# Linear attention with an ELU feed-forward behind it: one written order for the whole kernel, Strassen's products from block 2 on, blocks 8 and 9 transposed by DMA, block 0's keys loaded in long rows, products that nobody reads

## The chip, the cores and the metric

The kernel runs on one core of a Trainium2 chip. A core has a matrix engine (PE in the profile, with its weight loads as PEld), a vector engine (DVE), a scalar engine (ACT), a general engine (POOL) and a synchronising engine (SP), each with its own instruction stream that runs in order, and 16 DMA engines that all of them share. POOL's loads convert from fp32 to fp16 on the way. The metric is the device time in microseconds (us) of one execution; lower is better.

## The reference

Two things are computed one after the other. The first is attention with an exponential decay per head, in blocks of 64 tokens with a running state; q, k and v are 4 batches x 8 heads x 768 tokens x 64.

```python
for b in range(nb):                                   # 12 blocks of 64 tokens
    intra = einsum('bhic,bhjc->bhij', qb, kb) * Dmask
    intra = einsum('bhij,bhjd->bhid', intra, vb)
    inter = einsum('bhid,bhde->bhie', qb * lam_pow, kv_state)
    out[:, :, sl] = intra + inter
    kv_state = lam_block * kv_state + einsum('bhsd,bhse->bhde', kb * rev_pow, vb)
```

The second takes the 3072 x 512 result x and computes

```python
h = x @ w_in                                          # 512 -> 2048
g = where(h > 0, h, exp(min(h, 0)) - 1)
return g @ w_out                                      # 2048 -> 512
```

Both stages are fused: as soon as a block's attention is ready, its feed-forward can start.

## The kernel before, in words

The work is cut into 24 steps, numbered s: step s handles one block of 64 tokens for two batches, so 128 rows. "Block" in this document is such a step. Two blocks that follow each other form a group of 256 rows, 12 groups in all.

A block's attention is issued by `visit(so, us, ss, sx)`, which puts work of up to four blocks into the PE stream: for block ss the scores (`mm_S`), for us the update of the state (`mm_U`), for so the output (`mm_I` from the state in two halves, with a drain and the semaphore `crossed` between them, and `mm_O` from the scores), and for sx the transposes of q and k (`mm_T`, or the loop over `qn` and `kn` below it for the blocks under `NQ`, 6). Around it stand `att_C` (copies the transposed q and k from PSUM into the tile T), `att_P` (scores times mask), `att_N` (new state), `att_X` (attention output into xt), and three products with the decay: `decay_v` (tile vd), `decay_s` (sd) and `decay_q` (qs). From block `NT`, 10, on, the transposes are made by `dma_T` on SP's queue instead: two DMA transposes for a block, into one of two TD buffers.

The feed-forward's first product is cut into units (`mm1_h`) of one PSUM bank each, 8 matmuls of 256 columns or 16 of 128, into one of two banks psH. A unit's ELU is made by ACT (two activations, tiles e and r) and DVE (one operation, into g). The second product has two forms. `mm2` multiplies a block's g by w_out directly: 16 matmuls of 512 columns in four calls; it serves blocks 0 to 5. From group 3 on (block 6), Strassen's scheme takes 7 products for the two blocks of a group in place of 8 (`product_of`, called by `part`): each product is 8 matmuls of 256 columns. It needs sums of g (`g_sum`, four for a group, tiles s on DVE), sums of w_out made once (`w_sum`, tiles wt), and the products are put together by `keep` (a copy out of PSUM), `add` and `c2` (DVE).

Inputs come in through `load` on POOL's queue, in the order of the program; k, v and most q arrive as two DMAs of 64 KB with rows of 64 values, and q of blocks 0 to 5 in rows of eight tokens (`eights`), one DMA of 128 KB. Each of POOL's loads takes one of eight completion semaphores in turn, so a load's issue waits until the load eight places before it has landed. Block 0's k and q come in fp32 through SP's and ACT's queues and are cast (`cast0`). The weights w_in (`load_wi`, 8 DMAs) and w_out (`load_wo`, 4 DMAs) stand among these loads; from the second half of w_in's third quarter on they wait for `crossed`.

The order of all this is written out by hand: for the first part in the string `start`, whose words are each one step ("H0.0.1.0" is a unit of group 0, "M1.4" a quarter of block 1's second product, "A4.4.5.6" a visit), and from group 3 on in a loop over groups and their eight units. No scheduler moves anything: the program's order is the order on each engine.

Of the kernel before, what the change touches and what calls it, by code (L numbers as in the profile page):

```python
# [16 lines left out]
def kernel(  # L17
# [41 lines left out]

    NB = 12  # L60

    NT = 10

    NQ = 6
    kn, qn, vn = {}, {}, {}

    def eights(b, c):

        return q[b : b + 2, :, c * L : (c + 1) * L, :].rearrange("r h (p g) d -> (r h) p (g d)", g=8)

    def load(which, s):
        b, c = where(s)
        src, keep, tag = {"k": (k, kn, "kn"), "q": (q, qn, "qn"), "v": (v, vn, "vn")}[which]
        keep[s] = inp.tile([128, H, D], FP16, tag=tag, bufs=NB, name=f"{tag}{s}")
        if which == "q" and s < NQ:
            nc.gpsimd.dma_start(out=keep[s][:].rearrange("p h d -> p (h d)"), in_=eights(b, c))
            return
        for r in range(2):
            nc.gpsimd.dma_start(  # L79
                out=keep[s][half(r)],  # L80
                in_=src[b + r, :, c * L : (c + 1) * L, :].rearrange("h p d -> p h d"),
            )

    def load_step(s):
        load("k", s)
        load("q", s)
        load("v", s)
# [9 lines left out]
    def load_wi(i, halves=range(2)):  # L97

        for c in halves:
            ins = nc.gpsimd.dma_start(  # L100
                out=wi[i][half(c)],
                in_=moe_w_in[c * DM // 2 : (c + 1) * DM // 2, i * WB : (i + 1) * WB].rearrange(
                    "(g p) f -> p g f", p=64
                ),
            )
            if (i, c) == (2, 1):

                ins.wait_op(crossed, 1, "sem-ge")

    def load_wo(i):  # L110
# [3 lines left out]
        )  # L114

# [5 lines left out]
    for which, src in (("k", k), ("q", q)):  # L121
        raw0[which] = inp.tile([128, H, D], FP32, name=f"{which}raw0")
        if which == "q":
            nc.scalar.dma_start(out=raw0[which][:].rearrange("p h d -> p (h d)"), in_=eights(0, 0))
            continue
        for r in range(2):
            nc.sync.dma_start(
                out=raw0[which][half(r)], in_=src[r, :, 0:L, :].rearrange("h p d -> p h d")
            )
    load("v", 0)  # L130
    load_step(1)
    load_wi(0)
    load_step(2)
    load_wi(1)
    load_step(3)
    load_wi(2, [0])

# [95 lines left out]
    def att_C(s):  # L233
        if s >= NT:
            return
        T = asb.tile([128, 2, NHP, 2, L], FP16, tag="T", bufs=4, name=f"T{s}")
        psT = st[s].pop("psT")
        if s < NQ:
            nc.vector.tensor_copy(T[:, 0].rearrange("p j r t -> p (j r t)"), psT[0])
            nc.scalar.copy(  # L240
                out=T[:, 1].rearrange("p j r (t g) -> p (j r t) g", g=8),
                in_=psT[1].rearrange("p (g x) -> p x g", g=8),
            )
        else:
            nc.vector.tensor_copy(
                T[:].rearrange("p i j r t -> p r (i j) t"),
                psT.rearrange("p r (x t) -> p r x t", t=L),
            )
        st[s]["T"] = T

# [11 lines left out]
    def att_X(s, eng):  # L262
# [5 lines left out]
        if eng is nc.scalar:  # L268
            nc.scalar.copy(out=to, in_=O)
        else:  # L270
            eng.tensor_copy(to, O)
# [23 lines left out]
    def visit(so, us, ss, sx, begin=False):  # L295
# [23 lines left out]
        if sx is not None and sx < NQ:  # L319
            psT = st[sx]["psT"] = (psT[0][:, : NHP * L].bitcast(FP16), psT[1][:])  # L320
# [71 lines left out]
        if sx is not None and sx < NQ:  # L392
# [3 lines left out]
            for g in range(8):  # L396
                for x in range(2):
                    nc.tensor.matmul(
                        psT[1][half(x), g * 64 : (g + 1) * 64], lhsT=qn[sx][:, g, :], rhs=of[x],
                        start=True, stop=True, skip_group_check=True,  # L400
                    )
            for j in range(NHP):
# [32 lines left out]
    def mm1_e(grp, c0, nc_, n0):  # L435
# [4 lines left out]
        nc.scalar.activation(r[:], psH[:], AF.Relu)  # L440
# [22 lines left out]
    def elu(grp, u):  # L463

        psH, nb, T, name = unit[grp, 0, 2, u]
        if grp == 3 or grp == 4 and u < 6:
            mm1_e(grp, 0, 2, u)
            mm1_g(grp, 0, 2, u, NF2)
            return

        r = msb.tile([128, nb, T], FP32, tag="r", bufs=4, name=f"r{name}")
        nc.scalar.activation(r[:], psH[:], AF.Relu, scale=-1.0)  # L472
        e = msb.tile([128, nb, T], FP32, tag="e", bufs=4, name=f"e{name}")
        nc.scalar.activation(e[:], r[:], AF.Exp, scale=-1.0)  # L474
# [6 lines left out]
    nacc = [0]  # L481
# [8 lines left out]
    def mm2(s, n0):  # L490
        if n0 == 0:
            acc[s] = M[nacc[0] % 2][:]
            nacc[0] += 1
# [6 lines left out]
    def mm2_o(s):  # L500
        o = msb.tile([128, DM], FP32, tag="o", bufs=4, name=f"o{s}")
        nc.scalar.copy(out=o[:], in_=acc.pop(s))
# [56 lines left out]
    def part(grp, i):  # L559
        d = res.setdefault(grp, dict(A=M[0], B=M[1]))  # L560
        lo, hi = slice(0, HD), slice(HD, DM)
# [6 lines left out]
    def store(s, o, cols, queues=(nc.sync, nc.sync)):  # L568
        for r in range(2):
            queues[r].dma_start(out=rows(s, r)[:, cols], in_=o[half(r), cols])  # L570
# [7 lines left out]
    def keep(grp, tag, src, bufs=2):  # L578

        t = res[grp][tag] = msb.tile([128, *src.shape[1:]], FP32, tag=tag, bufs=bufs, name=f"{tag}_{grp}")  # L580
        nc.scalar.copy(out=t[:], in_=src)
# [5 lines left out]
    def c2(grp, queues=(nc.sync, nc.sync)):  # L587
# [5 lines left out]
        store(2 * grp + 1, d[1], slice(0, DM), queues)  # L593
# [12 lines left out]
    def later_loads():  # L606
        load_wi(2, [1])
        load_wo(0)
        load_wi(3)
        load_wo(1)  # L610
        load_wo(2)
        load("k", 4)
        load("q", 4)
        load_wo(3)
        load("v", 4)
        load_step(5)
        load_step(6)
        load_step(7)
        load_step(8)
        load("k", 9)  # L620
        load("q", 9)
        load("k", 10)
        load("q", 10)
        load("v", 9)
        load("k", 11)
        load("q", 11)
        load("v", 10)

    start = (
# [179 lines left out]
```

## Time and profile before

| what | us |
|---|---|
| timed runs | 205.8, 208.4, 208.91; median 208.4 |
| span of the profiled execution | 204.2 |
| the profiled execution's own time | its span; the profile shows nothing around it, and the timed runs are 1.6 to 4.7 longer |
| first matmul starts, last one ends | 6.5 and 200.1 |
| busy in the span: PE, DVE, ACT, POOL | 189.6, 168.7, 146.5, 123.4 |
| moved by DMA | 24.36 MB, of that 13.64 MB on POOL's queue |

How to read it: a busy time is the union of an engine's instructions, and PE's matmuls are pipelined with modelled ends, so short waits can hide in PE's busy time. The chain of waits follows the work that ended last back to the start. In the stretches between two times, "PEclk" is the clock that the throttle granted to PE.

### The profile page before, as it was taken

What the parts mean: (1) busy time and instruction counts of PE and PEld (TensorE: products, weight loads), DVE (VectorE), ACT (ScalarE), POOL (GpSimd) and SP (SyncE); (2) the same over time, 40 slices, a digit from 0 to 9 for tenths busy, and PEclk for the clock granted to TensorE, in tenths of its full rate; (3) what the DMA queues carried; (4) which work ended last, traced back from release to release, by engine and by line L of the source; (5) the groups of instructions that cost most, each with busy time, mean ns of one, the idle gap of its engine ahead of it and who ended that gap; (6) DMA issues with size and microseconds to landing.
All of it is one profiled execution on the core that took longest, in us unless ns stands there. A gap on an engine that the chain in (4) does not pass through costs nothing.

```text
span 204.2 us, 7590 instructions
## 1 busy us (share of the span) xinstructions
PE 189.6 (93%) x3216; PEld 156.6 (77%) x3216; DVE 168.7 (83%) x279; ACT 146.5 (72%) x283; POOL 123.4 (60%) x174
## 2 busy tenths in 40 slices
PE   0679899999999999999999989999999999999991
PEld 0457777647777777888888878888888888888881
DVE  4776996489989998999989999989979866758672
ACT  5626987635774879999878677788688788876820
POOL 8977832598998959997709999999222200020000
PEclk9999999999999999999999999999999999999998
DMA  6999999999999999999999999999915404004043
GB/s 102 157 171 171 152 206 196 180 124 156 117 148 150 173 108 172 153 134 78 74 163 109 206 105 86 185 111 105 169 27 69 94 0 108 0 6 100 3 103 103
DMA packets 94194, 24.36 MB, mean 119 GB/s; under 512 B 86160, under 2 KB 91152, under 8 KB 94160
## 3 DMA queue, kind: packets, MB, share of 16 engines
q0 software_dynamic: 73744, 13.64, 94.7%
q1 hardware_dynamic: 19968, 9.77, 26.9%
q10 hardware_dynamic: 448, 0.46, 1.0%
q8 instruction: 25, 0.41, 0.9%
q14 instruction: 9, 0.07, 0.1%
HBM read 27.27 MB, written 6.29 MB: 164 GB/s over the span
## 4 chain that ended last, share of the span: by engine, by line
PE 85%; DVE 4%; DMA 3%; POOL 3%; issue 2%; ACT 1%; POOLq 0%; DVEq 0%
PE psH L428 40%; PE psM L551 23%; PE psM L495 10%; DMA wi<-in_moe_w_in_dram 3%; PE psO_None L328 2%; POOL vn L79 1%; PE psZ L352 1%; PE psO_None L337 1%; PE psHB L551 1%; PE psHA L551 1%; DVE s L533 1%; PE psZ L344 1%; DVE g L475 1%; POOL kn L79 1%; PE psO L359 1%
## 5 line engine op out<-in xcount | busy, mean ns | idle before, releaser
L428 PE MATMUL psH<-xt,wi 128*128 128x256 f16 (+1 forms) x896 | 100.1, 261 | 1.9 <-ACT e L438 0.6
L428 PEld LDWEIGHTS <-wi 128*128 128x128 f16 x896 | 78.2, 100 | 13.3 <-issue 2.1
L475 DVE SCALAR_TENSOR_TENSOR g<-e,psH 128x512 f16<-128x512 f32 x58 | 39.6, 683 | 14.3 <-ACT e L474 13.8
L472 ACT ACTIVATE r<-psH 128x512 f32<-128x512 f32 x58 | 34.7, 598 | 18.3 <-PE psH L428 18.2
L474 ACT ACTIVATE e<-r 128x512 f32<-128x512 f32 x58 | 36.5, 630 | 1.8
L79 POOL DMA_DIRECT2D kn<-in_k_dram x46 | 32.2, 720 | 9.2 <-DMA wo<-in_moe_w_out_dram 5.1
L79 POOL DMA_DIRECT2D vn<-in_v_dram x48 | 34.1, 741 | 2.0 <-DMA wi<-in_moe_w_in_dram 1.1
L438 ACT ACTIVATE e<-psH 128x512 f32<-128x512 f32 x38 | 22.8, 601 | 14.7 <-PE psH L428 14.4
L551 PEld LDWEIGHTS <-s 128*128 128x128 f16 x288 | 28.1, 98 | 3.3
L445 DVE SCALAR_TENSOR_TENSOR g<-e,r 128x512 f16<-128x512 f32 x38 | 25.7, 685 | 4.1 <-ACT r L440 4.0
L220 POOL TENSOR_TENSOR qs<-TD,powi 128x512 f16<-128x512 f16 x11 | 13.9, 1264 | 19.3 <-PE psO_None L328 13.1
L79 POOL DMA_DIRECT2D qn<-in_q_dram x36 | 25.3, 735 | 0.0
L551 PE MATMUL psM<-wt,s 128*128 128x256 f16 x192 | 24.9, 273 | 0.0
L495 PE MATMUL psM<-wo,g 128*128 128x512 f16 x96 | 24.0, 379 | 0.0
L440 ACT ACTIVATE r<-psH 128x512 f16<-128x512 f32 x38 | 22.9, 602 | 0.0
L551 PEld LDWEIGHTS <-g 128*128 128x128 f16 x216 | 20.6, 98 | 2.6
L193 DVE TENSOR_TENSOR vd<-vn,rev 128x512 f16<-128x512 f16 x22 | 17.2, 783 | 1.8 <-DMA vn<-in_v_dram 1.7
L228 DVE TENSOR_TENSOR P<-psZ,mask 128x512 f16<-128x512 f32 x24 | 16.4, 684 | 2.0 <-PE psZ L344 1.1
L551 PE MATMUL psM<-wo,g 128*128 128x256 f16 x136 | 17.6, 272 | 0.0
L495 PEld LDWEIGHTS <-g 128*128 128x128 f16 x96 | 8.7, 98 | 7.0
L570 POOL DMA_DIRECT2D out_dram<-o x2 | 1.1, 574 | 21.1 <-DVE o L585 21.1
L533 DVE TENSOR_TENSOR s<-g 128x1024 f16<-128x1024 f16 x18 | 13.8, 764 | 0.0
(85 smaller groups left out, 228.7 us busy)
## 6 DMA issues: line engine op xcount, KB each, us to landing
out_dram<-o SPq DMA_DIRECT2D x43, 128.0 KB, 3.3
vn<-in_v_dram POOLq DMA_DIRECT2D x48, 64.0 KB, 5.0
kn<-in_k_dram POOLq DMA_DIRECT2D x46, 64.0 KB, 4.3
qn<-in_q_dram POOLq DMA_DIRECT2D x36, 64.0 KB, 4.5
wi<-in_moe_w_in_dram POOLq DMA_DIRECT2D x8, 256.0 KB, 8.9
wo<-in_moe_w_out_dram POOLq DMA_DIRECT2D x4, 512.0 KB, 12.6
qn<-in_q_dram POOLq DMA_DIRECT2D x5, 128.0 KB, 5.3
kraw<-in_k_dram SPq DMA_DIRECT2D x2, 128.0 KB, 4.7
```

The costliest lines, as they stand in the source:

```text
L79: nc.gpsimd.dma_start(out=keep[s][half(r)], in_=src[b + r, :, c * L : (c + 1) * L, :].rearrange("h p d -> p h d"),)
L193: eng.tensor_tensor(out=st[s]["vd"][:], in0=vn[s][:], in1=rev[:].unsqueeze(2).broadcast_to([128, H, D]), op=ALU.mult,)
L228: nc.vector.tensor_tensor(out=d["P"][:].rearrange("p y j t -> p y (j t)"), in0=psS, in1=mask[:].rearrange("p y j t -> p y (j t)"), op=ALU. ...
L428: nc.tensor.matmul(psH[:, i, :], lhsT=wi[n // 4][:, kk, (n % 4) * 128 : (n % 4 + 1) * 128], rhs=xt[grp][:, kk, c0 * 128 : c0 * 128 + T], s ...
L438: nc.scalar.activation(e[:], psH[:], AF.Exp)
L440: nc.scalar.activation(r[:], psH[:], AF.Relu)
L445: nc.vector.scalar_tensor_tensor(out=place(grp, c0, nc_, n0, nb, step), in0=e[:], scalar=-1.0, in1=r[:], op0=ALU.add, op1=ALU.min,)
L472: nc.scalar.activation(r[:], psH[:], AF.Relu, scale=-1.0)
L474: nc.scalar.activation(e[:], r[:], AF.Exp, scale=-1.0)
L475: nc.vector.scalar_tensor_tensor(out=place(grp, 0, 2, u, 2, NF2), in0=e[:], scalar=-1.0, in1=psH[:], op0=ALU.add, op1=ALU.max,)
L495: nc.tensor.matmul(acc[s], lhsT=g_of(s, n), rhs=wo[n // 4][:, n % 4, :], start=(n == 0), stop=(n == NFT - 1),)
L551: nc.tensor.matmul(to, lhsT=lhsT, rhs=rhs, start=start and n == 0, stop=stop and n == NF2 - 1, skip_group_check=True,)
```

## The change

One string `plan` replaces `start`, the loop over the groups and the code behind it. Its words carry the loads too ("lk4", "w2.1", "y0"), and flags that choose an engine: "V8.1" is decay_v on POOL, "X4.1" is att_X on DVE, "E1.0.1.0.1" and "e3.1.1" make ELU's first operation on DVE, "k1.p35.1" is a copy out of PSUM on DVE, "C4.1" copies the transposed k on ACT.

- Strassen's products ("p") start with group 1, so blocks 2 to 5 no longer use `mm2`; BANK fixes the PSUM bank of blocks 0 and 1.
- `NT` goes from 10 to 8: blocks 8 and 9 are transposed by DMA.
- Block 0's k is loaded in rows of eight tokens like q, as one DMA; its transposes take 16 matmuls in place of 4, and as the update of the state needs k in the other form, `rows_of_k` ("R0") transposes it back by four matmuls into a psH bank, and `copy_k` ("r0.0") copies that out.
- "Y2" and "Y4" are `unread`: 2 or 4 matmuls of 128 columns, identity by identity, into a part of a PSUM bank that is overwritten later. Ten stand before the first score products of block 0 or right around them, four later.
- The wait of `load_wi` for `crossed` is gone.

```diff
-    NT = 10
+    NT = 8
     NQ = 6
+    NK = 1
...
-        if which == "q" and s < NQ:
-            nc.gpsimd.dma_start(out=keep[s][:].rearrange("p h d -> p (h d)"), in_=eights(b, c))
+        if s < {"k": NK, "q": NQ, "v": 0}[which]:
+            nc.gpsimd.dma_start(out=keep[s][:].rearrange("p h d -> p (h d)"), in_=eights(b, c, src))
             return
...
-            if (i, c) == (2, 1):
-                ins.wait_op(crossed, 1, "sem-ge")
...
+    def unread(n):
+        for _ in range(n):
+            nc.tensor.matmul(
+                M[0][:, DM // 2 : DM // 2 + 128], lhsT=ident[:], rhs=ident[:],
+                start=True, stop=True, skip_group_check=True,
+            )
+    def rows_of_k(s):
+        bank = ps.tile([128, 512], FP32, tag="h", bufs=2, name=f"psK{s}")
+        to = st[s]["psK"] = bank[:, : NHP * L].bitcast(FP16)
+        for j in range(NHP):
+            nc.tensor.matmul(
+                to[:, j * 128 : (j + 1) * 128], lhsT=st[s]["T"][:, 0, j].rearrange("p r t -> p (r t)"),
+                rhs=ident[:], is_transpose=True, start=True, stop=True, skip_group_check=True,
+            )
...
-    def mm1_e(grp, c0, nc_, n0):
+    def mm1_e(grp, c0, nc_, n0, on_dve=0):
...
-        nc.scalar.activation(r[:], psH[:], AF.Relu)
+        if on_dve:
+            nc.vector.tensor_scalar_max(r[:], psH[:], 0.0)
+        else:
+            nc.scalar.activation(r[:], psH[:], AF.Relu)
...
     start = (
-        "Fq K0 Fk V0 A...0 C0 A.0.. K1 A..0. P0 A...1 N0 C1 A0... X0 V1 A..1. P1 A.1.. A1... X1 "
-        "N1 D2 H0.0.1.0 D3 E0.0.1.0 A...2 V2 C2 Q2 H0.1.1.0 A.2.2. I2 R P2 E0.1.1.0 A2... "
...
+    plan = (
+        "lk1 Y2 lv0 Fk Fq Y2 A...0 C0.0.1 Y2 K1 lq1 R0 Y4 lq2 w0.0 lv1 lk2 A..0. w0.1 lk3 lv2 "
+        "lq3 w1.0 K0 V0 w1.1 lv3 A...1 P0 C1 r0.0 A..1. A.0.. N0 V2.1 P1 w2.1 w2.0 A0... X0 V1 "
+        "D2 lq4 lk4 y0 A...2 C2.1 A.1.. V3.1 N1 A1... X1 w3.0 w3.1 lq5 D3.1 H0.0.1.0 E0.0.1.0 Q2 "
+        "lk5 H0.1.1.0 A.2.2. P2 E0.1.1.0 lk6 I2 A2... G0.0.1.0 N2 X2 A...3 H1.0.1.0 G0.1.1.0 "
+        "C3.0.1 H1.0.1.4 E1.0.1.0.1 H0.0.2.6 lv4 H0.0.2.4 Y2 lq6 Q3 I3 A.3.3. H0.0.2.8 D4 "
+        "E1.0.1.4 E0.0.2.6 G0.0.2.6 y1 P3 E0.0.2.4 G0.0.2.4 A3... H1.0.1.8 A...4 Y2 G1.0.1.4 y2 "
...
+        "G1.1.1.0 lq7 A4.4.5.6 H1.1.1.8 H1.0.2.12 M1.4 lv6 s1.3 E0.0.2.12 M0.4 X4.1 H2.0.1.0 P5 "
+        "B1.1 E1.1.1.8 G0.0.2.14 C6.1 lq8 Q6 G1.1.1.8 E1.0.2.12 E2.0.1.0 H2.0.1.8 E2.0.1.8 "
+        "G0.0.2.12 G1.0.2.12 s1.1 B2.0 M0.8 M1.8 H2.0.1.12 M1.12 B4.0 H2.0.1.4 M0.12 Z1 p1.2 "
+        "B2.1 B4.1 E2.0.1.4 k1.p2 V5 lv7 N4 A5.5.6.7 T8 p1.4 Z0 X5 B3.0 p1.5 s1.2 s1.4 P6 p1.1 "
...
+        "k11.c45.1 o21.0 p11.2 k11.u2 a11.3 p11.7 o22.1 c11 o23.3 o18.5 p11.3 a11.2 o22.2 "
+    )
```

Counted over the whole program, DVE goes from 279 instructions to 299, ACT from 283 to 266, and POOL's tensor operations from 19 to 31 (12 vd, 9 sd, 10 qs, where it was 8 sd and 11 qs). POOL's loads stay the same in number.

More of the change, by code (lines that the diff above doesn't have):

```diff
@@ L95, with load_wi @@
     crossed = tc.alloc_semaphore("crossed")
[L97 to L105, printed above, removed]
-            if (i, c) == (2, 1):
-                ins.wait_op(crossed, 1, "sem-ge")
+    def load_wi(i, c):
+        nc.gpsimd.dma_start(
+            out=wi[i][half(c)],
+            in_=moe_w_in[c * DM // 2 : (c + 1) * DM // 2, i * WB : (i + 1) * WB].rearrange(
+                "(g p) f -> p g f", p=64
+            ),
+        )
     def load_wo(i):
@@ L122 @@
         raw0[which] = inp.tile([128, H, D], FP32, name=f"{which}raw0")
[L123 to L136, printed above, removed]
+        eng = nc.scalar if which == "q" else nc.sync
+        eng.dma_start(out=raw0[which][:].rearrange("p h d -> p (h d)"), in_=eights(0, 0, src))
     ident = cst.tile([128, 128], FP16, name="ident")
@@ L267, in att_X @@
         O = st[s].pop("O").rearrange("p r (y t) -> p r y t", y=NHP)
[L268 to L271, printed above, removed]
+        copy(eng, to, O)
     def att_N(s):
@@ L395, in visit @@
             of = ident[:].rearrange("p (r j x t) -> x p j r t", r=2, j=NHP, x=2)
[L396 to L402, printed above, removed]
+            for i in (0, 1) if sx < NK else (1,):
+                for g in range(8):
+                    for x in range(2):
+                        nc.tensor.matmul(
+                            psT[i][half(x), g * 64 : (g + 1) * 64], lhsT=(kn, qn)[i][sx][:, g, :], rhs=of[x],
+                            start=True, stop=True, skip_group_check=True,
+                        )
+            for j in range(NHP) if sx >= NK else ():
                 nc.tensor.matmul(
@@ L480 @@
     acc = {}
-    nacc = [0]
+    BANK = (0, 1)
     def rows(s, r):
@@ L653 @@
     }
-    for word in start.split():
+    for word in plan.split():
         if word[0] == "A":
             visit(*(int(x) if x else None for x in word[1:].split(".")))
-        elif word[0] == "R":
-            later_loads()
+        elif word[0] in loads:
+            loads[word[0]](word[1:])
         elif word[0] == "F":
             cast0(word[1])
+        elif word[0] == "k":
+            grp, tag, *e = word[1:].split(".")
+            keep_of(int(grp), tag, *map(int, e))
+        elif word == "j":
+            last_banks()
```

266 lines of the change are left out of this document (93 added, 173 removed), and 53 rows, old and new, of tables (plan, start).

## The prediction

> **What bounds the kernel now.** I read the page's shares first, then the busy times by stretch, then the chain of waits, and last the groups. The page's first row and the stretches (us of each engine busy in each stretch):
>
> ```profile
> PE 189.6 (93%) x3216; PEld 156.6 (77%) x3216; DVE 168.7 (83%) x279; ACT 146.5 (72%) x283; POOL 123.4 (60%) x174
> ```
> ```profile
> 0.00:22.60 22.60, 13.51 (x309) 11.45 (x310) 15.33 (x35) 12.40 (x31) 18.79 (x34) 1.00 1.36 150
> 22.60:33.00 10.40, 9.47 (x161) 7.43 (x159) 8.33 (x15) 8.36 (x17) 4.37 (x7) 1.00 1.19 192
> ...
> 57.00:153.00 96.00, 95.47 (x1742) 79.90 (x1740) 89.80 (x142) 77.31 (x149) 77.90 (x103) 1.00 1.65 129
> 153.00:200.20 47.20, 47.11 (x600) 41.35 (x584) 34.94 (x59) 34.09 (x62) 3.48 (x4) 1.00 0.26 53
> ```
>
> The first number after each length is PE. From 57 us on it is idle for 0.53 + 0.09 us in 143: PE is the bound, and only less PE work shortens that part. Before 33 us it is idle 9.09 + 0.93 us, of which 6.5 pass before the first matmul; 3.5 us of idle time lie behind it. In 57 to 153 us DVE has 6.2 us to spare, POOL 18.1. The chain of waits (start, length, what) shows what PE does where:
>
> ```profile
> 7.01 6.18 DMA wi<-in_moe_w_in_dram
> 13.24 1.89 PE psH L428 x16
> 15.13 0.57 PE psM L398 x9
> 15.70 0.54 PE psM L403 x4
> 16.24 1.71 PE psH L428 x16
> ...
> 30.87 0.91 PE psH L428 x16
> 31.82 0.47 issue
> 32.29 0.60 ACT r L440
> 32.94 1.05 PE psH L428 x16
> 33.99 0.86 PE psM L495 x4
> ...
> 46.80 0.29 PE psO L359 x32
> ...
> 59.50 0.43 PE psO L359 x32
> ...
> 91.35 0.87 PE psM L551 x8
> 92.23 0.87 PE psH L428 x8
> 93.79 0.98 PE psH L428 x8
> ...
> 199.24 0.89 PE psHB L551 x8
> ```
>
> The first unit of the feed-forward waits until 13.24 for w_in's first quarter. The units of 128 columns then take 1.89 and 1.71 us where the same sixteen matmuls later take 0.91: PE runs at half its later pace until about 18 us, although the granted clock in the stretches reads 1.00 throughout. From 92.23 + 0.87 to 93.79 a visit costs 0.69.
>
> **The change, part by part.** Own time first: the profiled execution has a span of 204.2 and shows nothing around it; the median of the timed runs is 4.2 longer. I make the sum against 204.2 and add 4.2.
>
> *Strassen for groups 1 and 2.* Gone are 16 pieces like "33.99 0.86" (four matmuls of 512 columns; 4 blocks x 4): 13.8. New are 14 products like "91.35 0.87": 12.2. All of it is PE work in the part that PE bounds: **-1.6**. What comes with it lies on DVE and ACT, below.
>
> *Blocks 8 and 9 transposed by DMA.* Gone from PE are two of the pieces with 32 small transposes, 0.29 to 0.43 each, **-0.7**. New on SP are four DMA transposes; the rows of the ones that exist:
>
> ```profile
> TD<-kn SPq DMA_TRANSPOSE x14, 5.0
> TD<-qn SPq DMA_TRANSPOSE x14, 5.3
> ```
>
> They land 5.0 and 5.3 us after issue. In the plan block 8's stand nine PE units and a visit ahead of the visit that reads them, 9 x 0.87 + 0.69 = 8.5 us, and block 9's further; that hides them, and without that cover a visit would stand still for up to 5. On SP the stores of blocks 0, 2 and 3 queue between and behind these transposes; the o tile has four buffers, so nobody waits for them soon. Cost 0.
>
> *Block 0's keys.* Twelve more transposes, four back, and one more copy: about 1 us of PE by the rows "15.13 0.57" and "15.70 0.54", and a copy of some 0.4 on DVE. All of it comes before the first unit, where PE waits for the 6.18 us of "DMA wi". Cost 0; with that cover gone, 1.5.
>
> *Unread products.* Ten of them at the half pace (1.71 / 16 = 0.11) are 1.1 us, in the same wait. Four later ones at 0.06 cost **+0.2**. If they make PE reach its full pace before the first unit, the two units of 1.89 and 1.71 would take 0.91 each, -1.8 at best; if they only stand in the way, +1.1. I take 0: 1.1 us scattered over a wait of some 10 is little beside the 4.7 us (13.24 to 17.94) that PE worked without a pause before its pace doubled. The Trainium skill, page "TensorE: Matmul & The Clock Gate", section "Part 1: The HAM clock gate (the "warmup" mystery)", says that the array runs at half rate until it has been busy for about one window of 3.4 us, and that time counts, not the number of matmuls. By that rule this term is 0 as long as the gaps between the products stay; the trace agrees in the doubling.
>
> *The new order at the front.* Loads move in POOL's queue. Ahead of w_in's second half now stand also k of block 2 and q of block 2, 0.26 MB; at the 150 GB/s of the first stretch that is +1.7 for the first unit. The transposes of block 2, 0.57 + 0.54 = 1.1 at that place, now run before that unit: net +0.5. The weights of the second product come later as well. Before, their landings show in what POOL waited for (in brackets):
>
> ```profile
> 28.33 0.78 POOL L111 DMA_DIRECT2D wo<-in_moe_w_out_dram  x1 [2.67 <-DMA wo<-in_moe_w_out_dram]
> 33.38 0.68 POOL L79 DMA_DIRECT2D kn<-in_k_dram  x1 [1.62 <-DMA wo<-in_moe_w_out_dram]
> 40.66 1.35 POOL L79 DMA_DIRECT2D kn<-in_k_dram  x2 [1.66 <-DMA wo<-in_moe_w_out_dram]
> ```
>
> The first quarter of w_out landed at 28.3, the second at 33.4, the last at 40.7, and the piece "33.99 0.86" used the second at once: the front rode on its loads. After, five more loads of 0.13 MB and two q of the same size stand ahead of the second quarter: 0.92 MB at the 192 GB/s of the second stretch is 4.8 us, so it lands near 38. But the new order puts 16 units and 2 quarters of mm2 ahead of its first use where there were 13 and 2, and the transposes of blocks 4 to 6 with the visit of block 4: 3 x 0.9, and about 2.5 more by 0.57 + 0.54, 0.43 and 0.69, 5.2 us. Use and landing move together. What is left to win are the waits for ACT (0.93 idle in 22.6 to 33), as three of the early units get their second activation on DVE, and of the 2.6 us of idle time between the first matmul and 22.6 perhaps the half, 1.1. Term: +0.5 - 0.9 - 1.1 = **-1.5**; the ends are -3.0 (all 3.5 idle gone but the late start stays) and +1.5 (loads set the pace, nothing is won).
>
> A new wait stands on POOL: vd of block 2 is made there, and until v has landed w_in's third quarter, q and k of block 4 and w_out's first quarter queue behind it; block 0's eighth unit waits for the former. Before, vd2 stood on DVE. Cost 0 to 1.5, held in the +1.5.
>
> *DVE, ACT and POOL.* The rows:
>
> ```profile
> L193 DVE TENSOR_TENSOR vd<-vn,rev 128x512 f16<-128x512 f16 x22 | 17.2, 783 | 1.8 <-DMA vn<-in_v_dram 1.7
> L533 DVE TENSOR_TENSOR s<-g 128x1024 f16<-128x1024 f16 x18 | 13.8, 764 | 0.0
> L585 DVE TENSOR_TENSOR o<-psM,p 128x256 f32<-128x256 f32 x15 | 6.3, 418 | 0.4
> L245 DVE COPY T<-psO 128x1024 f16<-128x1024 f16 x4 | 2.7, 679 | 0.0
> L220 POOL TENSOR_TENSOR qs<-TD,powi 128x512 f16<-128x512 f16 x11 | 13.9, 1264 | 19.3 <-PE psO_None L328 13.1 <-PE psM L551 6.1
> ```
>
> DVE gains 8 sums at 0.764, 4 adds at 0.418, 2 c2 and 11 operations taken over from ACT (nearest row: 0.679), 10 copies out of PSUM (nearest: 0.418): 6.1 + 1.7 + 8.8 + 4.2 = 20.8. It loses 12 vd at 0.783 and four copies at 0.679: 12.1. Net +8.7 on 168.7. POOL gets 12 vd; no row shows one there, so between DVE's 0.783 and the 1.264 of qs on POOL, from which I take 1.2: +14.4, and one operation's balance of sd and qs. In 57 to 153 us, where POOL has 18.1 to spare, it fits. ACT loses some 8. And POOL and DVE disturb each other:
>
> ```profile
> 113.26 1.59 POOL L220 TENSOR_TENSOR qs<-TD,powi 128x512 f16<-128x512 f16 x1
> 114.90 1.51 DVE L533 TENSOR_TENSOR s<-s,g 128x1024 f16<-128x1024 f16 x1
> 120.08 1.58 DVE L193 TENSOR_TENSOR vd<-vn,rev 128x512 f16<-128x512 f16 x1
> ```
>
> The sum and the vd that meet a tensor operation on POOL take 1.51 and 1.58 in place of 0.68. Over the 36 sums and 22 vd the excess is about 36 x 0.08 + 22 x 0.10 = 5.1 us, 0.27 for each of POOL's 19 tensor operations; 12 more make +3.2. So DVE goes to about 181 of 201 us. Where it runs out, PE waits, as in the 0.53 above. I take **+0.5**, from -0.5 (the old wait goes) to +3.
>
> Sum: -1.6 - 0.7 + 0.2 - 1.5 + 0.5 = -3.1; span 201.1, time **205.3**. What follows "199.24 0.89" is the same as before: a sum on DVE and the last stores.
>
> **The rivals.** *A better front (faster).* PE gets to its full pace before the first unit (-1.8), one more microsecond of the 3.5 idle goes, and DVE's +0.5 doesn't come: -3.1 - 1.8 - 1.0 - 0.5 = -6.4, time 202.0. For it speaks that ten products, 32 transposes and three more visits' work now stand close in the first wait; against it the gaps for ACT's and DVE's copies between them.
>
> *The front is bound by its loads (no change).* Then the order wins nothing, +1.5 in place of -1.5: -0.1, time 208.3. For it speaks that three of the four landings of w_out were waited for; against it that the use moves back as far.
>
> *POOL and DVE shut each other out (slower).* If two in three of POOL's 31 tensor operations meet a sum, a vd or a qs on DVE at +0.83 (1.51 - 0.68), that is 17 us on DVE in place of 5.1, +12; with the +8.7 it is past the 6.2 that DVE has free in 57 to 153 and the rest of its room, so some 10 of it reach PE: -3.1 - 0.5 + 10 = +6.4, time 214.8. It decides once the meetings outnumber about 0.4 for each operation of POOL. The present 0.27 / 0.83 is 0.33 and speaks against it. The Trainium skill, page "SBUF — State Buffer", section "Who interferes with whom", states this as an exclusive lock for a DVE operation with two SBUF inputs against a POOL one that reads SBUF; the 1.51, 1.58 and 1.59 agree.
>
> **How the numbers follow.** Forecast 0.46, better front 0.30, bound by loads 0.13, shut out 0.11. A measurement of this kernel tells about 2% from no change, here 204.2 and 212.6. Of the forecast's 0.46 I put 0.08 under 204.2. Faster 0.30 + 0.08 = 0.38; within 2% 0.38 + 0.13 = 0.51; slower 0.11. The range holds the first three cases: from 200.8 (every term at its lower end: -1.6 - 0.9 + 0.2 - 1.8 - 3.0 - 0.5 = -7.6) to 210 (the loads as bound, 208.3, and half of DVE's +3).
>
> **What would show it.** Right: 77 products in place of 63 on PE and 8 pieces of mm2; transposes on PE for blocks 0 to 7 only; the first unit at 13.5 to 15; w_out's second quarter landing near 38 without PE idle for it; PE idle under 1 us from 57 on; DVE near 181 busy. Wrong: PE idle for DVE's g or s in many places, sums with a mean over 0.9, or a first unit after 16.

## The result, and the profile after

| what | before | after |
|---|---|---|
| timed runs, median (lowest to highest), us | 207.5 (205.8 to 208.9) | 221.2 (220.6 to 221.8) |
| ratio, 95% interval | | 1.0739 (1.0696 to 1.0782) |
| span of the profiled execution | 204.2 | 218.9 (its time 220.6) |
| last matmul ends | 200.1 | 214.5 |

The change makes the kernel 7.4% slower. The forecast was 205.3 with a range to 210.0, so the result lies far outside, beyond the one rival on that side too (214.8). Times here and below are medians of all executions; the ratios and their intervals leave out the executions that were over 1.5% slower than the fastest of the same kernel, so a ratio can differ a little from the quotient of two medians.

The page's first row, and the busy times by stretch (start:end, length, then PE, PEld, DVE, ACT and POOL with their instructions, granted clock, DMA share, GB/s), both of the kernel after:

```profile
PE 192.9 (88%) x3230; PEld 163.3 (75%) x3230; DVE 190.5 (87%) x299; ACT 140.9 (64%) x266; POOL 139.6 (64%) x186
```
```profile
0.00:22.60 22.60, 14.29 (x330) 12.08 (x331) 14.57 (x33) 11.07 (x28) 19.62 (x35) 1.00 1.31 147
22.60:33.00 10.40, 9.28 (x185) 7.60 (x185) 10.16 (x15) 7.77 (x15) 8.59 (x13) 1.00 1.51 181
33.00:57.00 24.00, 22.73 (x475) 17.64 (x473) 23.20 (x40) 16.35 (x30) 16.25 (x24) 1.00 1.60 145
57.00:70.00 13.00, 11.07 (x175) 9.70 (x175) 11.24 (x15) 6.86 (x14) 12.03 (x16) 1.00 1.73 127
70.00:90.00 20.00, 16.00 (x260) 12.78 (x261) 20.00 (x24) 11.73 (x25) 19.67 (x24) 0.91 1.32 98
90.00:153.00 63.00, 59.56 (x992) 51.19 (x980) 56.61 (x89) 47.32 (x89) 46.37 (x60) 1.00 1.25 119
153.00:214.60 61.60, 59.94 (x841) 52.33 (x840) 54.31 (x89) 39.86 (x68) 17.03 (x20) 1.00 0.50 75
```

PE's idle time, length less busy, is 8.3 + 1.1 + 1.3 us up to 57 and 1.9 + 4.0 + 3.4 + 1.7 = 11.0 from there on, where it was 0.6 before. The largest of PE's waits for DVE from 57 us on (who waited for what: total, times, longest) make up some 8 of these 11.0:

```profile
PE psM L637 <- DVE s L619: 3.5, 2, 2.9
PE psH L501 <- DVE g L562: 2.8, 4, 1.3
PE psZ L424 <- DVE P L267: 1.1, 1, 1.1
PE psM L637 <- DVE o L674: 0.9, 2, 0.6
```

PE's busy time is 3.3 longer, and of that up to 20 x 0.09 = 1.8 is the clock of 0.91 in 70 to 90. In those 20 us DVE is busy without a gap, and yet does 24 instructions. Why it takes so long shows in DVE's groups (count, then total busy and mean ns of one) and POOL's:

```profile
L562 DVE SCALAR_TENSOR_TENSOR g<-e,psH 128x512 f16<-128x512 f32 x58 | 39.5, 682 | 8.0 <-ACT e L554 7.6
L521 DVE SCALAR_TENSOR_TENSOR g<-e,r 128x512 f16<-128x512 f32 x38 | 33.1, 893 | 0.1
L619 DVE TENSOR_TENSOR s<-g 128x1024 f16<-128x1024 f16 x22 | 15.0, 684 | 0.2
L619 DVE TENSOR_TENSOR s<-g,s 128x1024 f16<-128x1024 f16 x11 | 13.1, 1187 | 0.0
L619 DVE TENSOR_TENSOR s<-s,g 128x1024 f16<-128x1024 f16 x11 | 9.3, 843 | 0.2
L250 DVE TENSOR_TENSOR sd<-st,lamL 128x512 f32<-128x512 f16 x8 | 7.9, 990 | 0.0
...
L232 POOL TENSOR_TENSOR vd<-vn,rev 128x512 f16<-128x512 f16 x12 | 14.7, 1225 | 0.7 <-DVE T L276 0.5
```
```profile
L521 DVE SCALAR_TENSOR_TENSOR g<-e,r 128x512 f16<-128x512 f32 x22 | 21.9, 1008 | 0.0
```

The ELU's last operation exists in two forms. The one that reads its second operand from PSUM (psH) takes 0.68, as before. The one that reads both from SBUF (e and r) takes 0.89 in the mean, and 1.01 in the stretch from 50 to 122 us (second fence); before it took the same 0.68 in all 38 cases. Sums of the form s<-g read SBUF only as well and still have a mean of 0.68 (22): four of them overlap one of POOL's products in the timeline, three that had begun 0.06 to 0.23 us before it and one that met its last 0.15. One place in the timeline, DVE, POOL and PE:

```profile
77.81 1.52 DVE L521 SCALAR_TENSOR_TENSOR g<-e,r 128x512 f16<-128x512 f32 x1
79.26 2.62 DVE L619 TENSOR_TENSOR s<-g,s 128x1024 f16<-128x1024 f16 x1
...
77.37 1.42 POOL L250 TENSOR_TENSOR sd<-st,lamL 128x512 f32<-128x512 f16 x1 [0.33 <-DVE st L353]
78.74 1.40 POOL L135 DMA_DIRECT2D vn<-in_v_dram  x2
80.14 1.18 POOL L259 TENSOR_TENSOR qs<-TD,powi 128x512 f16<-128x512 f16 x1
...
77.94 1.05 PE L501 MATMUL psH<-xt,wi 128*128 128x256 f16 x8
81.94 1.19 PE L637 MATMUL psM<-wo,s 128*128 128x256 f16 x8 [2.95 <-DVE s L619]
82.91 3.48 PE L501 MATMUL psH<-xt,wi 128*128 128x256 f16 x16
```

A g and a sum in a row stand beside POOL's sd and qs, 1.52 and 2.62 in place of 0.68; PE waits 2.95 for the sum, and soon after does sixteen matmuls in 3.48 where they take 1.92 elsewhere (at 102.29, say).

### The profile page after: what moved, and what is told of

It is laid out like the page before. It is cut to its first block, busy times and chain, and to the rows that moved or that the text cites. A ratio compares the mean times of both kernels' runs of the same rounds, so it can differ in the third digit from the quotient of the medians.

```text
span 218.9 us, 7630 instructions
## 1 busy us (share of the span) xinstructions
PE 192.9 (88%) x3230; PEld 163.3 (75%) x3230; DVE 190.5 (87%) x299; ACT 140.9 (64%) x266; POOL 139.6 (64%) x186
## 4 chain that ended last, share of the span: by engine, by line
PE 46%; DVE 20%; DMA 19%; POOL 5%; issue 5%; ACT 3%; SPq 0%; DVEq 0%; POOLq 0%
PE psH L501 23%; PE psM L637 17%; DVE g L521 5%; DVE s L619 5%; DMA wo<-in_moe_w_out_dram 5%; DMA kn<-in_k_dram 5%; DMA wi<-in_moe_w_in_dram 4%; DMA vn<-in_v_dram 3%; DVE g L562 2%; DVE P L267 2%; DMA out_dram<-o 2%; POOL qn L135 2%; POOL vn L135 1%; PE psO_None L400 1%; DVE st L353 1%
## 5 line engine op out<-in xcount | busy, mean ns | idle before, releaser
L637 PEld LDWEIGHTS <-s 128*128 128x128 f16 x352 | 34.1, 98 | 9.3 <-DVE s L619 4.1
L511 ACT ACTIVATE e<-psH 128x512 f32<-128x512 f32 x38 | 22.8, 601 | 20.9 <-PE psH L501 13.5
L521 DVE SCALAR_TENSOR_TENSOR g<-e,r 128x512 f16<-128x512 f32 x38 | 33.1, 893 | 0.1
L637 PE MATMUL psM<-wt,s 128*128 128x256 f16 x240 | 31.1, 273 | 0.9 <-DVE o L674 0.9
L637 PEld LDWEIGHTS <-g 128*128 128x128 f16 x264 | 25.5, 98 | 3.4
L250 POOL TENSOR_TENSOR sd<-st,lamL 128x512 f32<-128x512 f16 x9 | 11.9, 1320 | 18.0 <-DVE st L353 18.0
L637 PE MATMUL psM<-wo,g 128*128 128x256 f16 x168 | 21.8, 273 | 0.0
L516 ACT ACTIVATE r<-psH 128x512 f16<-128x512 f32 x33 | 19.8, 601 | 0.0
L259 POOL TENSOR_TENSOR qs<-TD,powi 128x512 f16<-128x512 f16 x9 | 12.1, 1349 | 5.9 <-DMA TD<-qn 5.8
L232 POOL TENSOR_TENSOR vd<-vn,rev 128x512 f16<-128x512 f16 x12 | 14.7, 1225 | 0.7 <-DVE T L276 0.5
L353 DVE TENSOR_TENSOR st<-psZ,sd 128x512 f16<-128x512 f32 x20 | 13.6, 682 | 0.3 <-PE psO_None L400 0.3
```

Source lines behind the costliest of these rows:

```text
L353: nc.vector.tensor_tensor(out=to, in0=psU, in1=st[s]["sd"][:].rearrange("p y j d -> p y (j d)"), op=ALU.add)
L511: nc.scalar.activation(e[:], psH[:], AF.Exp)
L521: nc.vector.scalar_tensor_tensor(out=place(grp, c0, nc_, n0, nb, step), in0=e[:], scalar=-1.0, in1=r[:], op0=ALU.add, op1=ALU.min,)
L637: nc.tensor.matmul(to, lhsT=lhsT, rhs=rhs, start=start and n == 0, stop=stop and n == NF2 - 1, skip_group_check=True,)
```

## The experiments

Three theories went in. **A**: DVE's operations with two SBUF inputs stand still while POOL multiplies, and PE waits for DVE. **B**: DVE has too much work of its own in this order. **C**: the loads, and POOL's queue as their way, set the pace of the front. Each run is compared with runs of the kernel before on the same chip, whose medians lay between 205.1 and 205.8; the runs stand on several chips, so differences between two of them are safer by their ratios than by their times.

**POOL's products replaced by fills.** In the kernel after, all 31 of POOL's `decay_v`, `decay_s` and `decay_q`:

```diff
-        eng.tensor_tensor(out=out, in0=in0, in1=in1, op=ALU.mult)
+        nc.gpsimd.tensor_tensor(out=out[..., 0:1], in0=in0[..., 0:1], in1=in1[..., 0:1], op=ALU.mult)
+        nc.gpsimd.memset(out[..., 1:64], 0.0)
```

> The kernel after, but where POOL multiplies (vd, sd, qs, 31 times) it multiplies one column only and fills the other 63 with zeros, which reads no SBUF; the waits for the inputs stay, and the decay is left out of those blocks. Theory A (DVE operations with two SBUF inputs stand still while POOL's tensor operations run): the 19.4 us that DVE's groups stand above their undisturbed 0.68 go, DVE is busy for 170 to 175 in place of 190.5, the groups g<-e,r and s<-g,s come to a mean of 0.68 to 0.75, and the time is 205 to 211. Theory B (DVE simply has too much of its own work in this order, 7.5 us more): the time stays at 216 to 222. Theory C (the loads, and POOL's queue as their way, set the pace up to 60 us): 216 to 221.

Measured: 206.7, ratio 1.0048 (1.0001 to 1.0094), so 14.5 us less than the kernel after (by the ratios 6.9%, 14.2). The page's first row, three groups, and the stretches:

```profile
PE 189.7 (93%) x3230; PEld 162.7 (80%) x3230; DVE 171.6 (84%) x299; ACT 140.7 (69%) x266; POOL 124.1 (61%) x217
```
```profile
L584 DVE SCALAR_TENSOR_TENSOR g<-e,psH 128x512 f16<-128x512 f32 x58 | 39.7, 685 | 10.6 <-ACT e L576 10.2
L543 DVE SCALAR_TENSOR_TENSOR g<-e,r 128x512 f16<-128x512 f32 x38 | 25.2, 686 | 1.4 <-ACT r L538 1.4
...
L641 DVE TENSOR_TENSOR s<-g,s 128x1024 f16<-128x1024 f16 x11 | 7.5, 685 | 0.0
```
```profile
0.00:22.60 22.60, 14.79 (x330) 12.54 (x331) 14.23 (x33) 11.03 (x28) 19.75 (x38) 1.00 1.31 151
22.60:33.00 10.40, 10.02 (x194) 8.21 (x194) 9.13 (x16) 8.17 (x16) 7.33 (x13) 1.00 1.52 176
33.00:57.00 24.00, 23.13 (x482) 17.98 (x480) 23.07 (x39) 16.27 (x31) 16.97 (x26) 1.00 1.74 151
57.00:153.00 96.00, 95.38 (x1625) 83.45 (x1623) 85.88 (x147) 75.28 (x144) 72.79 (x129) 1.00 1.45 123
153.00:199.50 46.50, 46.43 (x607) 40.57 (x604) 38.91 (x68) 29.94 (x51) 7.21 (x14) 1.00 0.45 79
```

With the same 299 instructions DVE is busy 18.9 us less, 0.61 for each of POOL's 31 operations, and each form with two SBUF inputs is back at 0.68. PE's idle time from 57 on falls from 11.0 to 0.7. That is theory A, and B and C expected no gain of this size. But the fills also make POOL faster (139.6 to 124.1 busy), so its products are ready earlier and its loads leave earlier.

**The same POOL, with and without reading.** To the kernel with fills one unread operation is added behind each fill: a multiplication of 128 x 512 from SBUF, or a fill of 1024 columns.

```diff
         nc.gpsimd.memset(out[..., 1:64], 0.0)
+        nc.gpsimd.tensor_tensor(out=spare, in0=powi, in1=ones, op=ALU.mult)   # first kernel
+        nc.gpsimd.memset(spare, 0.0)                                          # second kernel
```

> The kernel after with fills, and behind each of the 31 fills one POOL multiplication of 128 x 512 from SBUF into a tile that nobody reads. POOL's own products are ready as early as with the fills, and nobody waits for the unread ones. Theory A: DVE's operations with two SBUF inputs stand still again, busy 183 to 192, the time is 214 to 222. If what cost the time was that POOL's products came late: 206 to 210.

> The same with one more fill of 1024 columns (about 1.1 us, it reads nothing) in place of each unread multiplication, so POOL and the loads queued behind it are as busy. Theory A: DVE stays at 171 to 173, the time is 206 to 209. If POOL's busy queue and its later loads cost the time: 212 to 220, as with the multiplications.

Measured: 223.6 with the multiplications, ratio 1.0872 (1.0806 to 1.0937); 209.2 with the fills, 1.0186 (1.0127 to 1.0245). Page row and groups, first of the multiplications:

```profile
PE 197.2 (88%) x3230; PEld 165.0 (74%) x3230; DVE 196.9 (88%) x300; ACT 141.2 (63%) x266; POOL 163.4 (73%) x248
...
L588 DVE SCALAR_TENSOR_TENSOR g<-e,psH 128x512 f16<-128x512 f32 x58 | 39.4, 680 | 5.4 <-ACT e L580 5.0
L547 DVE SCALAR_TENSOR_TENSOR g<-e,r 128x512 f16<-128x512 f32 x38 | 32.0, 864 | 0.4 <-ACT r L542 0.4
L238 POOL TENSOR_TENSOR spare<-powi,ones 128x512 f16<-128x512 f32 x31 | 38.6, 1245 | 0.0
```

and of the fills:

```profile
PE 191.0 (92%) x3230; PEld 163.2 (78%) x3230; DVE 171.8 (82%) x299; ACT 141.1 (68%) x266; POOL 151.8 (73%) x248
...
L545 DVE SCALAR_TENSOR_TENSOR g<-e,r 128x512 f16<-128x512 f32 x38 | 25.2, 684 | 1.3 <-ACT r L540 1.3
L236 POOL MEMSET spare<- 128x1024 f16 x31 | 44.5, 1437 | 0.0
```

Nobody waits for these operations. By POOL's busy time the fills add 27.7 us (124.1 to 151.8), 0.89 each, and the multiplications 39.3, 1.27 each; the fills' mean of 1437 ns is in records that overlap others. So POOL is not quite as full with the fills. A POOL fuller by 27.7 costs 2.5 us (206.7 to 209.2), so the further 11.6 would cost about 1 at that rate (an estimate from these two runs). The multiplications cost 14.4 more than the fills, and put 25.1 us onto DVE, 0.81 for each operation; by DVE's groups the forms with two SBUF inputs carry all of it (25.4), and the form with psH takes 0.68 in both. This settles A against "POOL is late", but for that 1. The Trainium skill, page "SBUF — State Buffer", section "Who interferes with whom", says that a DVE instruction with two SBUF inputs contends with a GpSimd instruction that reads SBUF, not with one that only writes it. All four kernels so far agree with it: among the forms that DVE repeats from block to block, wherever a mean stands clear of its undisturbed time, both inputs lie in SBUF and POOL multiplies.

**The kernel before with its own 19 products as fills.** The same edit there.

> The kernel before with its 19 decay products on POOL made as one column times decay and a fill with zeros (the decay is left out there). It tells what POOL's tensor operations cost before: theory A expects DVE to lose the 5 us above 0.68 (busy 163 to 165) and PE its wait near 120 us, 0.5 to 1; the time is 204 to 206. Then the rest of the change, without POOL's part, is the difference between 206.7 of the kernel after with fills and this time: 0 to +2.5. Theory C would have no change, 205 to 207.

Measured: 204.8, ratio 0.9974 (0.9933 to 1.0016); DVE 164.2, PE idle 0.1 + 0.4 us from 57 on. Before, POOL cost next to nothing. So without POOL's part the rest of the change costs 206.7 - 204.8 = 1.9 (by the ratios 0.7%, 1.5, and as the intervals lie anything from 0 to 3), against the 3.6 that the prediction's sum had as its gain.

**One part alone: twelve vd on POOL, in the kernel before.**

```diff
+        if s == 2 or 11 <= s <= 21:
+            eng = nc.gpsimd
         st[s]["vd"] = asb.tile([128, H, D], FP16, tag="vd", bufs=3, name=f"vd{s}")
```

> The kernel before with one edit: the vd of block 2 and of blocks 11 to 21, 12 as in the kernel after, are made on POOL. Theory A: DVE loses 12 x 0.78 = 9.4 us of work but meets 12 more tensor operations of POOL at some 0.63 each, 7.6 us; busy 165 to 170, and as the meetings come in front of PE's waits the time is 209 to 215. Theory B: DVE is relieved by 9.4, the time is 205 to 208.5.

Measured: 211.3, ratio 1.0251 (1.0185 to 1.0317), with DVE at 165.1. DVE is relieved by 3.6 us and the kernel is 1.9 to 3.2% slower. The stretches, and the timeline of DVE, POOL and PE, show one place where it is lost:

```profile
85.00:100.00 15.00, 12.73 (x217) 10.31 (x216) 12.31 (x16) 10.65 (x24) 14.24 (x19) 0.89 1.88 111
100.00:153.00 53.00, 53.00 (x885) 46.48 (x883) 45.41 (x70) 42.83 (x80) 47.39 (x58) 1.00 1.26 124
```
```profile
86.44 1.89 DVE L535 TENSOR_TENSOR s<-g 128x1024 f16<-128x1024 f16 x1
88.26 0.41 DVE L587 TENSOR_TENSOR o<-psM,p 128x256 f32<-128x256 f32 x1
88.59 1.19 DVE L447 SCALAR_TENSOR_TENSOR g<-e,r 128x512 f16<-128x512 f32 x1
...
90.91 1.30 DVE L447 SCALAR_TENSOR_TENSOR g<-e,r 128x512 f16<-128x512 f32 x1
...
87.66 1.57 POOL L195 TENSOR_TENSOR vd<-vn,rev 128x512 f16<-128x512 f16 x1
...
94.06 1.86 PE L430 MATMUL psH<-xt,wi 128*128 128x256 f16 x8 [2.27 <-DVE g L477]
95.72 1.78 PE L553 MATMUL psM<-wo,s 128*128 128x256 f16 x8
```

Beside POOL's new vd, and a qs at 86.53 just ahead of it, a sum and a g take 1.21 and 0.51 us more than 0.68, and a later g 0.62 more, where the records show only loads on POOL; PE stands for 2.27, and then does two pieces in 1.86 and 1.78 that otherwise take 1.04. In the stretch 2.27 is idle and up to 15 x 0.11 = 1.65 is the clock.

**DVE relieved otherwise.** In the kernel after, the flags for POOL are taken back (all 31 products on DVE), or the flags that moved work from ACT to DVE (23 words), or both, or both but for vd of blocks 2 and 3:

```diff
-... V8.1 ... D10.1 ... Q7.1 ...      +... V8 ... D10 ... Q7 ...        (products to DVE)
-... X4.1 ... k1.p35.1 ... e3.1.1 ... +... X4 ... k1.p35 ... e3.1 ...   (copies and ELU to ACT)
```

> The kernel after with all 31 decay products on DVE, none on POOL. Theory A: 19.4 us of standing still are exchanged for 31 x 0.68 = 21.1 us of work, DVE stays at 190 to 194 busy and the time at 217 to 225. Theory B: 21 us more on an engine that is already the bound, 228 to 240. Theory C: POOL's loads no longer stand behind tensor operations, 212 to 217.

> The kernel after with the 23 operations that its flags moved from ACT to DVE (attention output, copies out of PSUM, first ELU operations, two copies of q) back on ACT; POOL as it is. Theory A: DVE's own work falls by 12 to 13, its standing still stays at 15 to 20, busy 176 to 180; the time is 211 to 217. Theory B: the 7.5 us too many are gone, 206 to 210. Theory C: 217 to 221.

> The kernel after with all 31 decay products on DVE and the 23 moved copies and first ELU operations back on ACT. Theory A: no standing still is left (it was 19.4 us), DVE's work is 189.0 - 12.5 = 176 to 178, below the 183 of PE's work and 13 less than where the time was 221.9; the time is 206 to 213. If the order itself, or DVE's place ahead of PE's waits, is what is too tight (theory B): above 216.

> The kernel with all decays on DVE and the copies on ACT (220.0), but vd of blocks 2 and 3 on POOL as in the kernel after. In that kernel DVE waited 4.0 us in order for v of a block to land and PE 5.2 for that vd. Theory: this wait is what it lost first, the time is 214 to 217, and what is left above 207 is DVE being late in many places. If the early wait was covered anyway: 219 to 221.

| products on | copies on | DVE busy | time | ratio (interval) |
|---|---|---|---|---|
| DVE | DVE, as in after | 189.0 | 221.9 | 1.0795 (1.0740 to 1.0849) |
| POOL, as in after | ACT | 179.7 | 221.9 | 1.0810 (1.0758 to 1.0862) |
| DVE | ACT | 177.5 | 220.0 | 1.0716 (1.0657 to 1.0774) |
| DVE, vd of 2 and 3 on POOL | ACT | 176.7 | 216.0 | 1.0544 (1.0492 to 1.0596) |

The first came as theory A had it (DVE at 189.0, just under the 190 that it expected): 18.9 us of standing still or 21 of work is the same. The second and the third did not: DVE's busy time falls by 11 and 13 us and the time stays. A sum over DVE's time is no account of the kernel; it counts where in the order DVE is late. One such place shows in the third kernel's waits (who waited for what: total, times, longest):

```profile
DVE vd L232 <- DMA vn<-in_v_dram: 5.7, 2, 3.9
...
PE psZ L416 <- DVE vd L232: 5.2, 1, 5.2
```

vd of an early block stands in DVE's queue until v has landed, and everything behind it waits. With those two on POOL PE no longer waits 5.2 there, and the fourth kernel gets 4.0 back, as expected. The 9 us that still lie between it and the 206.7 of the kernel with fills are not settled: none of the forms with two SBUF inputs stands above 0.69 there, DVE has 5 us more work and ACT 9, and PE is idle 8.1 us from 57 on where it was 0.7, in short waits, most of them for DVE and ACT (the longest 1.3). The fills leave the decay out, so their 206.7 is no time that this plan could have: the 31 products cost as much on DVE as they do on POOL, and of the kernels here that keep the plan with its decay, 216.0 is the lowest.

**Which of POOL's products.** Fills for the 10 products of blocks up to 10 only, or for the 21 of later blocks only.

```diff
-        if eng is nc.gpsimd:
+        if eng is nc.gpsimd and s <= 10:     # or: s > 10
```

> The kernel after with the fills in place of POOL's tensor operations for blocks up to 10 only (10 of the 31; the decay is left out there), the later 21 as they are. The excess of DVE in after lies mostly where the form g<-e,r is (a mean of 1.01 us in 50 to 122 us). Theory A: the 10 early ones carry about 9 of the 14.5 us, the time is 210 to 214. If the price goes by the number of operations, 14.5 x 10/31 = 4.7, 215.5 to 218.

> The counterpart: fills for the 21 decay products of blocks 11 on, the first 10 on POOL as tensor operations. Theory A: these carry about 5, the time is 214.5 to 218. If the price goes by the number, 9.8, 210 to 213. The two gains together should make 14.5 if one stall does not hide another.

Measured: 215.7, ratio 1.0560 (1.0498 to 1.0623), where the 21 late ones still multiply; 214.9, ratio 1.0447 (1.0382 to 1.0513), where the 10 early ones do. Above the 1.0048 of all fills the 10 early ones alone cost 4.0% and the 21 late ones 5.1%, 0.8 and 0.5 us for each; both together cost 6.9%. An early one costs more, but that the early ones carry most of it was wrong. Nor is it shown that the form g<-e,r makes the difference: its mean is 0.79 with the early ones and 0.82 with the late ones. The two gains, 5.5 and 6.3, make 11.8 and not 14.5, so one delay hides part of another.

**Small parts.** Blocks 8 and 9 transposed by DMA in the kernel before (NT = 8, with "T8" and "T9" behind the visits of blocks 5 and 6); the kernel after with fills and without the 14 unread products; and the same kernel with fills with w_in's first quarter and the first unit moved ahead of block 2:

```diff
-    NT = 10                                  +    NT = 8
-... Fq Y2 A...0 C0.0.1 Y2 K1 lq1 R0 Y4 ...   +... Fq A...0 C0.0.1 K1 lq1 R0 ...
-... lq2 w0.0 lv1 lk2 A..0. w0.1 lk3 ...      +... lv1 w0.0 w0.1 A..0. lq2 lk2 lk3 ...
-... A...2 C2.1 A.1.. ... H0.0.1.0 E0.0.1.0   +... A.1.. ... H0.0.1.0 E0.0.1.0 A...2 C2.1
```

> The kernel before with NT = 8 alone: blocks 8 and 9 transposed by DMA, issued one visit after the visit that uses block 6 and block 7. Two pieces of 32 transposes leave PE and two copies of 0.68 leave DVE; the sum of the prediction has -0.7, the time 204.5 to 206. If the transposes land late (5.0 and 5.3 us after issue, behind two stores): 206.5 to 210.

> The kernel after with the fills on POOL, without the 14 unread products. By the prediction's sum: the ten first ones cost 0 and the four later ones 0.2, so 206 to 207. If they make PE reach its full pace earlier, 207.5 to 209; if the ten stand in the way, 205 to 206.

> The kernel after with fills, but w_in's first quarter loaded ahead of q and k of block 2, and the first unit ahead of block 2's transposes, as in the kernel before. The first unit starts at 13.0 to 13.5 in place of 14.5. If the late start is what the new front lost: 205.0 to 206.0. If block 2's own loads now hold the front: 206.5 to 208.5.

Measured: NT = 8 alone 209.2, ratio 1.0121 (1.0047 to 1.0195), so 1 to 4 us slower where -0.7 was expected. That is the expectation's case of transposes that land late, and in its profiled execution, the longest of the six (213.2), PE waits 2.6 for a transposed q (TD<-qn) and 3.0 for a load of q, neither of which before has. Whether these waits are the 1 to 4 us of the shorter executions isn't shown. Without the unread products 207.1, ratio 1.0068 (1.0032 to 1.0103) against 1.0048: no difference that these runs can tell. With the first unit ahead 207.3, ratio 1.0091 (1.0058 to 1.0123): no gain; but the unit then started at 14.26 and not at 13.0 to 13.5, as block 1's vd held PE for 1.78, so this run doesn't test what it was meant to.

## Why the prediction was wrong, point by point

*What bounds the kernel.* Right for before, and the 6.2 us that DVE had to spare in 57 to 153 were the right place to look. What the reading left out: these 6.2 are a sum, and a DVE that is 2 to 3 us late in one place can cost PE more than that.

*Strassen: -1.6.* Right. All of PE's groups of the second matmul with L637 together are 616 matmuls, 77 products, with 79.9 us busy where it was 65.3, and what is left of `mm2` has 7.9 where it was 24.0: -1.5. That PE's busy time with the fills (189.7) still equals that before (189.6) comes from the unread products (2.2 in their group) and block 0's keys, which add about what Strassen and the two blocks' transposes take away.

*DMA transposes: 0 for the transposes, -0.7.* PE's groups of 32 small transposes fell from 2.8 to 1.4, so -1.4 was there to take. No PE wait in the kernel after names the DMA transposes, as priced. But in the old order they came with 1 to 4 us, and in the new order PE waits 1.0 for one where POOL has the unread fills and 1.3 where all products are on DVE and the copies on ACT, so the cover of 8.5 us is not a safe one.

*Block 0's keys and the unread products: 0 and +0.2.* Not refuted: the runs without the unread products show no difference, and in the kernel after the pace still doubles near 18 us (two units of 128 columns in 3.41 us at 14.79, in 1.95 at 20.38).

*The new order: -1.5.* Not reached, and not for POOL's products. With the fills PE's idle time up to 57 is 7.8 + 0.4 + 0.9 = 9.1; before it was 9.1 + 0.9 in the two stretches quoted there and none in the third, whose row is

```profile
33.00:57.00 24.00, 24.00 (x437) 16.45 (x437) 19.84 (x33) 14.31 (x27) 18.82 (x29) 1.00 1.54 151
```

so 10.0: 0.9 were won. The waits for ACT went, as priced (0.9 to 0.4 in 22.6 to 33). But the first unit started at 14.54 with the fills and 14.79 in the kernel after, 1.3 and 1.55 later than before where +0.5 was booked (the range 13.5 to 15 holds), and 0.9 of new idle time stands in 33 to 57. In the new order block 2's transposes stand ahead of that unit, and PE waits there for block 2's k, 1.25 us in the kernel after (at 13.60). Without the unread products it waits 1.74 there and starts the unit at 15.02, so they are not what made it late. In this place a load sets the pace, which the second rival had for the whole front; for w_out PE waits once, 0.2 us, and use and landing did move together.

Of everything but POOL and DVE -3.6 was expected and some +1.9 measured against the kernel before with fills. Where the 5 us between went is known in part only: PE's busy time, which was to fall by 2.1, stayed (the unread products and block 0's keys were booked as hidden), and 0.9 us of idle time went where 1.5 were booked. The rest can't be told from the difference between executions: the profiled one with fills has a span 0.4 shorter than the one before (203.8 and 204.2).

*DVE, ACT and POOL: +0.5, from -0.5 to +3.* This step failed, in its term for the collisions. Its list was right: DVE's work without collisions rose from 164.2 to 171.6, +7.4 (predicted +8.7), and vd on POOL takes 1.225 (taken as 1.2). Its collisions were not: +3.2 predicted, and 18.9 - (168.7 - 164.2) = +14.4 measured. The prediction took the excess of 0.27 us per POOL operation from before (by the run with fills 4.5 / 19 = 0.24) and multiplied it by twelve more. That rate came from a kernel in which POOL's multiplications began when the ELU form with two SBUF inputs was nearly over, as the source line's range and POOL's first multiplication show there:

```profile
L445 DVE SCALAR_TENSOR_TENSOR g<-e,r x38: 674/683/694, 19.1 to 87.7; 128x512 f16<-128x512 f32 x38
...
83.51 1.57 POOL L220 TENSOR_TENSOR qs<-TD,powi 128x512 f16<-128x512 f16 x1
```

Of these 38 DVE operations one stands beside a multiplication there, and it had begun 0.13 us before it (at 83.38, 0.68 long). So 38 operations that can collide hardly had the chance, and the prediction's list of what can collide left them out. In the new plan POOL multiplies at 16.6, 22.2 and 25.0 and from 60.7 on, while this form runs from 19.2 to 100.4, and the rate is 0.61. The rule of the Trainium skill, page "SBUF — State Buffer", section "Who interferes with whom", that the prediction cited would have put this form on the list: it goes by the operands, and e and r both lie in SBUF.

What the collisions did to the time can be added up between the kernel after and the one with fills, by their spans (218.9 and 203.8, 15.1): PE's idle time from 57 on is 10.3 longer, its idle time before that 1.6, and its busy time 3.2, of which up to 1.8 is the lower clock in 70 to 90. Of the signs that the prediction named, the 77 products and the first unit's start held; PE's idle time from 57 on (11.0 for under 1) and DVE's busy time (190.5 for 181) went against it. The sums' mean of 0.85 stayed under the 0.9 that was to be the warning, as the form g<-e,r carried much of the delay and was not watched.

*The rival "POOL and DVE shut each other out": 214.8, chance 0.11.* The mechanism was this one, with its chance set too low and its price too. It allowed for meetings with s, vd and qs only, two in three at 0.83 each, and let 10 of 17 us reach PE. In fact 14.5 us of time go with 18.9 us on DVE. (The sum at 114.90 among its lines met POOL's sd at 114.83, not the qs shown above it, which ended at 114.85.)

*From span to time: +4.2.* Too large by some 2.5: the profiled executions take 1.7 to 1.8 more than their spans (220.6 for 218.9 after, 205.6 for 203.8 with fills), and the median of before was 205.4 in 23 later runs, so the 208.4 was the chance of three.

## What to carry to other kernels

When work moves to an engine whose operations make another's stand still, price it by the operands of what will run beside it after the change, not by the rate of collisions before: an operation that shows its clean duration may only never have met the other engine. Here DVE's forms with one operand in PSUM were free beside POOL, and those with both in SBUF were not when they began while POOL was multiplying: on average 0.24 us of DVE time for each POOL multiplication before, 0.61 after, 0.81 with the unread ones. And a bound that rests on an engine's total spare time is weak where that engine stands directly ahead of PE: in the kernel before with twelve vd on POOL, 2.3 us of lateness in the operations shown were followed by 2.27 of idle PE and up to 1.65 of lower clock.

## What the runs showed that was not expected

- A DVE operation can stand longer than POOL's operation lasts. The sum at 79.26 took 2.62, and ended 0.56 after POOL's qs (80.14 + 1.18), although it had begun 0.88 before that qs by the records, while POOL was issuing two loads; the g at 90.91 in the kernel before with twelve vd on POOL is another such case. Loads alone don't do it, as with the fills, where POOL issues the same loads, and with all products on DVE, where it does nothing else, all these forms take 0.68 to 0.69. Of eleven sums and g in the kernel after that began ahead of a POOL product that they overlap, six took 0.68 to 0.78 and five 0.97 to 2.62. Why those five didn't finish first isn't settled; POOL's records are rough.
- A PE that stands for 2.27 or 2.95 us can fall to half its pace (1.86 for 1.04, 3.48 for 1.92), and the granted clock of the stretch shows it (0.89 in 85 to 100, 0.83 in 80 to 90). It needn't: in the kernel with fills for blocks up to 10 PE stands 2.35 at 81.0 and keeps its pace (sixteen matmuls in 1.92). And up to 18 us the pace is half at a granted clock of 1.00. The Trainium skill, page "TensorE: Matmul & The Clock Gate", section "Part 1: The HAM clock gate (the "warmup" mystery)", gives about 3.4 us of idle time for that; the traces show it after less.
- DVE operations that follow each other without a gap start every 0.60 us though each is recorded with 0.68 (76.01, 76.61, 77.21 in the timeline of after), so the busy time of a full DVE is that of 0.60 steps.
